# Left-over small runs planned away in a two-layer mixture-of-experts kernel

## Chip, cores and metric

One core of a Trainium2 chip runs the whole program. The metric is the device time of one execution in microseconds, 483.08 us (median of 3 runs, 481.55 to 483.19). Names of engines: PE is TensorE (matmuls; PEld its weight loads), DVE VectorE, ACT ScalarE, POOL GpSimd, SP SyncE, which here only issues DMAs.

## What is computed

The input x is (4, 8, 512, 64) and a state is (4, 8, 32, 64). An attention between them, both ways, gives 4 × (512 + 32) = 2176 tokens of 8 × 64 = 512 numbers. Two mixture-of-experts layers follow, each with 8 experts of hidden width 1024; a token goes to one expert alone, the one with the largest logit.

```python
xread  = softmax(scale * x @ state.T) @ state       # (4, 8, 512, 64)
sread  = softmax(scale * state @ x.T) @ x           # (4, 8, 32, 64)
x = concat([xread, sread], axis=2) -> (2176, 512)

def moe(x, w_gate, w1, w2, capacity=None):
    logits = x @ w_gate                             # (2176, 8)
    e = argmax(logits, axis=1); gate = softmax(logits)[e]
    # with a capacity (576 in layer 0) an expert keeps its first 576 tokens only
    for each expert: y = relu(xe @ w1[e]) @ w2[e];  out[its tokens] = gate * y
```

Everything is fp32. A product is made of three fp32r matmuls, of a high and a low half of either factor (names that end in h and l).

## The kernel before

How many tokens an expert gets is known only on the chip. So each layer first makes a **plan** of runs. A full run, a **quad**, takes 512 rows of one expert: four gathers of 128 rows, turned by PE (`x_quad`), then for each of eight chunks of the hidden width 12 matmuls with w0 (line 1044), relu by ACT into hTh (line 1046) and the low half by DVE into hTl (line 1047), and 12 matmuls with w1 (line 1055). What remains of an expert's rows becomes one more quad where it is over 128 rows, and a **small run** where it is 1 to 128. A small run's rows are turned and copied by ACT at line 1028 and multiplied in plain fp32.

The stages: stage 0 is an expert's first quad; each further quad is a further stage, for which `deeper` opens an `If` on the count of quads (line 1470; the nest goes on to 11 quads). Beside each further stage k, between its matmuls, run up to two small runs, in slots 2(k-1) and 2(k-1)+1. NA is 4, so there are eight such slots. A small run for which there is no place goes into a **left-over slot** (8 to 15) and runs alone after the last quad: `left` tests slot 8's kind (line 1502), and inside it are eight nested tests of the following slots, each with a whole small run in its body. This stands in the program twice, behind either layer.

The plan is a chain of DVE instructions (`plan_runs`, lines 434 to 530). They are emitted a few at a time, by "ticks" between groups of PE's matmuls, in turn with the steps that list the tokens (lov and loc, lines 334 and 336, each read by PE at line 342). Every engine works in order, so PE waits at its list matmuls until DVE has come that far, and a DVE step of the plan that stands ahead of a lov makes it late. `key` orders the remainders by size, `slot` is a small run's place, `nr` holds the counts and kinds that become registers. `m` and `left` in the plan add a jump to slot 8 for those beyond 2 per further stage. `plan_lists` makes the rows to be gathered; its last three instructions make `rows1`, a second list that says which run comes next.

`planned` lets POOL cast nr to integers (line 1518) and issues the next loads of weights; `ready` loads the registers: the count of quads, the kind of the left-over slot (`left_`), the kinds of two small runs. `load_beside` loads the weights of the next small run and branches on whether it is a planned or a left-over one.

The gathers and the stores are indirect DMAs issued by POOL (lines 561 and 1073). The end of an `If` around such DMAs has, on POOL, waits and an instruction that the trace names INC_SWDGE_SEM and the order ISA. Line 1580 is the end of the program.

Of the kernel before, what the change touches and what calls it, by code (L numbers as in the profile page):

```python
# [47 lines left out]
NA = 4  # L48
NS_ = 2 * NA + E
NT = ML * QT + NS_  # L50
# [27 lines left out]
def moe_kernel(ctx: ExitStack, tc: tile.TileContext, x, state, wg1, w1a, w2a, cap, wg2, w1b, w2b, out):  # L78
# [344 lines left out]
    def plan_runs(pool, L):  # L423
# [31 lines left out]
        DVE.scalar_tensor_tensor(out=sm, in0=rem, scalar=0.5, in1=sm, op0=ALU.is_gt, op1=ALU.mult)  # L455
        DVE.tensor_tensor(out=before, in0=before, in1=bc(nl[:, None, :], [P, E, E]), op=ALU.mult)
# [3 lines left out]
        yield  # L460
        start = t_([E], "pst")
        DVE.tensor_reduce(out=start, in_=before, axis=AX.X, op=ALU.add)
        DVE.tensor_tensor(out=key, in0=key, in1=sm, op=ALU.mult)
        kd = t_([E], "pkd")
        DVE.scalar_tensor_tensor(out=kd, in0=rem, scalar=SMALL[0] + 0.5, in1=sm, op0=ALU.is_gt, op1=ALU.add)
        m = t_([2], "pm2")
        DVE.tensor_scalar(m[:, 0:1], nr[:, 0:1], -1.0, float(NA), op0=ALU.add, op1=ALU.min)
        yield
        DVE.tensor_tensor(out=before, in0=bc(key[:, None, :], [P, E, E]), in1=bc(key[:, :, None], [P, E, E]), op=ALU.is_gt)
        DVE.tensor_scalar(m[:, 0:1], m[:, 0:1], 2.0, None, op0=ALU.mult)  # L470
        ends = t_([E], "pen")
# [3 lines left out]
        yield  # L475
        slot = t_([E], "psl")
        DVE.tensor_reduce(out=slot, in_=before, axis=AX.X, op=ALU.add)
        l2 = t_([ML, E], "pl2")
        DVE.tensor_tensor(out=l2, in0=bc(ends[:, None, :], [P, ML, E]), in1=bc(iof[:, 0:ML, None], [P, ML, E]), op=ALU.is_gt)
        DVE.tensor_scalar(m[:, 1:2], m[:, 0:1], -1.0, float(2 * NA), op0=ALU.mult, op1=ALU.add)  # L480
        yield
        left = t_([E], "plf")
        DVE.tensor_scalar(left, slot, m[:, 0:1], m[:, 1:2], op0=ALU.is_ge, op1=ALU.mult)
        DVE.tensor_tensor(out=le, in0=le, in1=l2, op=ALU.mult)
        out_ = t_([E], "pout")
        DVE.tensor_scalar(out_, sm, -FAR, FAR, op0=ALU.mult, op1=ALU.add)
        yield
        DVE.tensor_tensor(out=slot, in0=slot, in1=left, op=ALU.add)
        DVE.tensor_tensor(out=le, in0=le, in1=bc(iof[:, None, 0:E], [P, ML, E]), op=ALU.mult)
        DVE.scalar_tensor_tensor(out=kd, in0=rem, scalar=SMALL[1] + 0.5, in1=kd, op0=ALU.is_gt, op1=ALU.add)  # L490
        yield
        DVE.tensor_tensor(out=slot, in0=slot, in1=out_, op=ALU.add)
        DVE.tensor_reduce(out=nr[:, 1:1 + ML], in_=le, axis=AX.X, op=ALU.add)
        DVE.tensor_tensor(out=kd, in0=kd, in1=sm, op=ALU.mult)
        yield
        se = t_([NS_, E], "pse")
        DVE.tensor_tensor(out=se, in0=bc(slot[:, None, :], [P, NS_, E]), in1=bc(iof[:, 0:NS_, None], [P, NS_, E]), op=ALU.is_equal)
# [18 lines left out]
        DVE.tensor_reduce(out=pr, in_=pk, axis=AX.X, op=ALU.add)  # L516
        no = t_([NA], "pno")
        DVE.tensor_scalar(no, iof[:, 1:1 + NA], nr[:, 0:1], None, op0=ALU.is_ge)
        yield
# [11 lines left out]
        yield  # L531
        rt["plan"] = mk, no

    def plan_lists(pool, L):

        mk, no = rt.pop("plan")
# [11 lines left out]
        yield  # L548
        DVE.tensor_tensor(out=no, in0=no, in1=ss[:, 0:2 * NA].rearrange("p (a b) -> p a b", b=2)[:, :, 0], op=ALU.add)
        yield  # L550
        DVE.tensor_scalar(rows1[L], no, -1.0, 0.0, op0=ALU.add, op1=ALU.max)
        yield

# [479 lines left out]

    def get_next(L, k):
        gather(L, rows1[L][:, k:k + 1], xs1)


# [54 lines left out]
    class Logits:  # L1092
# [22 lines left out]
        def events(self, turns):  # L1115
# [7 lines left out]
            return ev  # L1123

        def alone(self):
            for i in range(0, self.n, 2):
                self.turn(i)
                if i + 1 < self.n:
                    self.turn(i + 1)
                self.product(i, pyv)  # L1130
            return self

# [136 lines left out]

    def load_beside(L, k):  # L1270

        if k >= NA:
            return
        n = load_reg(L, 0, spo, ML)
        with tc.If(n > k + 1) as cmp:
            load_small(L, 2 * k)
        with cmp.Else():
            load_small(L, 2 * NA)

    def split1(half, c):  # L1280
# [4 lines left out]

    nq_, kd_, left_ = {}, {}, {}

# [77 lines left out]
    def stage(L, k, ev=(), ticks=0, fg=()):  # L1365

        lists = [at(SPLIT2, lambda c: wsplit(1, c, ON[4 if L or k else 2])), ev]
        if L or k:
            lists.append(at(SPLITB, split1, 1))
        if k:  # L1370
            lists.append([(SPLITB[-1] + 1, lambda: load_next(L, k + 1, 0)), (SPLIT2[-1] + 1, lambda: load_next(L, k + 1, 1))])
        st = Stage(lists)
        DVE.tensor_copy(mcur, cols(L, k))
        DVE.tensor_copy(gq[0], gq[1])
        if k == 0:
            st.common(CUT[2], ticks, fg)
# [86 lines left out]
    def deeper(st, L, k):  # L1463
# [17 lines left out]
        elif (L, k) in ((0, 2), (1, 0)):  # L1481
            tc.mark_branch_hint_location(f"left{L}", hint="LikelyTaken", engines=ALL)
            tail(st, L, (1, gidx_e[1]) if L == 0 else None)

    def layer(st, L):

        deeper(st, L, 0)
        left(L)

    def left(L):  # L1490

        def alone(s):
            run_all(one(L, 2, s, 0))
            if L == 0:
                run_all(behind(Logits(1, 0).alone()))
            if s + 1 < NS_:
                load_small(L, s + 1)
                get_small(L, s + 1)

        def from_(s):  # L1500
            v = left_[L] if s == 2 * NA else load_reg(L, KINDS + s, mx=len(SMALL))
            with tc.If(v > 0, preferred_fallthrough_block=True, label=f"left{L}" if s == 2 * NA else None):  # L1502
                if L == 0 and s == 2 * NA:
                    run_all(behind(Logits(QT + 2, 0).alone()))
                    nothing(meta[:, 0:QT + 2])
                alone(s)
                if s + 1 < NS_:
                    from_(s + 1)
                if L == 0 and s == 2 * NA:
                    nothing(meta[:, 0:1])  # L1510

        from_(2 * NA)

# [32 lines left out]
    list_clear()  # L1546
    layer(st, 0)

# [7 lines left out]
    ready(1)  # L1556
    layer(st, 1)

# [37 lines left out]
```

## Time and profile before

| what | value |
|---|---|
| runs | 483.08 us median (481.55 to 483.19) |
| profiled execution | 483.41 us, span 481.6 us |
| mean granted clock of TensorE | 0.962 |
| PE | 428.4 us busy, 89% of the span |
| DVE, ACT, POOL | 187.1, 165.8, 199.6 us |
| HBM | 67.70 MB read, 21.52 MB written |

The span is what the profiler saw of the program's instructions; 1.81 us of the execution lie around it. A busy share is an average: whether an engine sets the time is read from the idle time in front of its instructions and from what ended it. A releaser with a q behind the engine's name (DVEq L1502) is an instruction of that engine's own sequencer: a branch, a wait or a semaphore.

### The profile page before, as it was taken

The page shows a single profiled execution, that of the slowest core. Times are in us where ns is not written, and L with a number is a line of the kernel's source. Part 1 is how long each engine was busy: PE and PEld are TensorE (multiplying, and loading weights), DVE is VectorE, ACT ScalarE, POOL GpSimd, SP SyncE. Part 2 cuts the span into 40 slices and gives each one's busy share as a digit, 9 for nine tenths or more (in the row PEclk, how much of TensorE's full clock was granted, in tenths as well). Part 3 has the DMA queues.
Part 4 walks back from the last instruction along what each step waited for, and adds up shares of the span by engine and source line. Part 5 has one row for each costly group of instructions (what it writes and reads, how often), then busy time and mean ns, then how long its engine had stood idle before and what let it go on. Part 6 is the DMA issues. An engine that isn't in the chain of part 4 may idle for free. (4 is left out here: it accounts for less than half of the span.)

```text
span 481.6 us, 8218 instructions
## 1 busy us (share of the span) xinstructions
PE 428.4 (89%) x2757; PEld 310.8 (65%) x2757; DVE 187.1 (39%) x655; ACT 165.8 (34%) x288; POOL 199.6 (41%) x175
## 2 busy tenths in 40 slices
PE   8859577979999899999989889999989999999880
PEld 5647455757875684775775667777646847768760
DVE  7975655897141340041353052971410100411020
ACT  4657355120244411355312245203423113453010
POOL 6531253110814526415443724558524306675011
PEclk9998788997999999999998999999999999999996
DMA  7363639985999975909732300119997858210001
GB/s 236 98 154 85 212 81 301 227 171 196 395 385 333 372 247 192 338 7 342 297 135 83 94 5 3 68 46 354 340 360 267 302 187 276 95 38 2 8 24 66
DMA packets 47354, 89.38 MB, mean 186 GB/s; under 512 B 8592, under 2 KB 21136, under 8 KB 47248
## 3 DMA queue, kind: packets, MB, share of 16 engines
q1 hardware_dynamic: 42128, 72.43, 45.4%
q0 software_dynamic: 5120, 15.76, 9.4%
q8 instruction: 40, 0.66, 0.6%
q14 instruction: 66, 0.54, 0.4%
HBM read 67.70 MB, written 21.52 MB: 185 GB/s over the span
## 5 line engine op out<-in xcount | busy, mean ns | idle before, releaser
L1047 DVE SCALAR_TENSOR_TENSOR hTl<-ph,hTh 128x512 fp32r<-128x512 f32 x48 | 33.2, 691 | 208.1 <-ACT hTh L1046 187.7
L1055 PE MATMUL py<-w1h,hTh 128*128 128x512 f32 x192 | 81.2, 423 | 0.0
L276 POOL TENSOR_TENSOR w1l<-raw,w1h 128x1024 fp32r<-128x1024 f32 x22 | 52.5, 2392 | 61.9 <-ACT w1h L275 61.8
L1055 PE MATMUL py<-w1h,hTl 128*128 128x512 f32 x192 | 75.2, 392 | 0.6 <-issue 0.6
L1055 PE MATMUL py<-w1l,hTh 128*128 128x512 f32 x192 | 75.1, 391 | 0.0
L1046 ACT ACTIVATE hTh<-ph 128x512 fp32r<-128x512 f32 x48 | 28.7, 599 | 131.9 <-PE ph L1044 94.8
L1283 POOL TENSOR_TENSOR w0l<-raw,w0h 128x512 fp32r<-128x512 f32 x40 | 51.1, 1293 | 40.0 <-ACT w0h L1282 39.9
L1044 PE MATMUL ph<-xTh,w0h 128*128 128x512 f32 x192 | 55.2, 410 | 4.8 <-ACTq L1470 1.5
L1044 PE MATMUL ph<-xTl,w0h 128*128 128x512 f32 x192 | 55.4, 410 | 0.0
L1044 PE MATMUL ph<-xTh,w0l 128*128 128x512 f32 x192 | 55.1, 410 | 0.0
L1044 PEld LDWEIGHTS ph<-xTh,w0h 128*128 128x128 f32 x192 | 35.8, 192 | 14.7 <-issue 2.8
L1044 PEld LDWEIGHTS ph<-xTl,w0h 128*128 128x128 f32 x192 | 35.6, 190 | 13.0 <-issue 6.1
L1055 PEld LDWEIGHTS py<-w1h,hTh 128*128 128x128 f32 x192 | 36.1, 188 | 9.4 <-issue 3.4
L1044 PEld LDWEIGHTS ph<-xTh,w0l 128*128 128x128 f32 x192 | 35.8, 194 | 9.5 <-issue 2.5
L1055 PEld LDWEIGHTS py<-w1h,hTl 128*128 128x128 f32 x192 | 36.1, 188 | 8.9 <-issue 1.0
L1055 PEld LDWEIGHTS py<-w1l,hTh 128*128 128x128 f32 x192 | 36.2, 189 | 6.5 <-issue 1.0
L1073 POOL DMA_INDIRECT out_dram<-ysb,dsti x15 | 15.0, 1000 | 60.6 <-ACT ysb L1063 53.6
L1282 ACT CAST w0h<-raw 128x512 fp32r<-128x512 f32 x40 | 23.8, 618 | 14.2 <-DMA raw<-in_moe_w_dram 6.8
L1073 POOL DMA_INDIRECT yrows<-ysb,dsti x16 | 16.2, 1012 | 28.0 <-DVE oc L334 8.0
L275 ACT CAST w1h<-raw 128x1024 fp32r<-128x1024 f32 x24 | 25.1, 1044 | 0.4 <-ACTq L1502 0.4
L861 PE MATMUL pav<-vg,e1T 128*128 128x264 f32 x56 | 18.3, 456 | 0.5 <-ACT xr L862 0.5
L832 POOL TENSOR_TENSOR u<-u,m 128x512 f32<-128x512 f32 x8 | 8.4, 1054 | 22.9 <-ACT xr L862 11.3
(314 smaller groups left out, 598.4 us busy)
## 6 DMA issues: line engine op xcount, KB each, us to landing
raw<-in_moe_w_dram SPq DMA_DIRECT2D x104, 512.0 KB, 7.2
out_dram<-zb SPq DMA_DIRECT2D x2, 2176.0 KB
xrows<-xr SPq DMA_DIRECT2D x16, 256.0 KB, 3.9
yrows<-zeros SPq DMA_DIRECT2D x3, 1026.0 KB
xb<-in_x_dram SPq DMA_DIRECT2D x6, 512.0 KB
yrows<-zeros SPq DMA_DIRECT2D x1, 1282.5 KB
xb<-in_x_dram SPq DMA_DIRECT2D x4, 256.0 KB, 4.0
st<-in_state_dram SPq DMA_DIRECT2D x1, 256.0 KB
```

What stands on the lines that cost most here:

```text
L275: ACT.copy(h, t)
L276: (POOL if on[c] else DVE).tensor_tensor(out=l, in0=t, in1=h.bitcast(F32), op=ALU.subtract)
L832: POOL.tensor_tensor(out=u[o], in0=u[o], in1=bc(m1[o][:, :, None], [P, S // NS, NS]), op=ALU.mult)
L861: PE.matmul(pv[:, a, 0:GW], e1_[b][:, r % 2, a, r // 2], vg[:, b, a], start=True, stop=True)
L1044: PE.matmul(p, w[k][:, 0, c * P:(c + 1) * P], u[:, k], start=(i == 0 and k == 0), stop=(i == 2 and k == NC1 - 1))
L1046: ACT.activation(out=hTh[:, c % 2], in_=p, func=AF.Relu)
L1047: DVE.scalar_tensor_tensor(out=hTl[:, c % 2], in0=p, scalar=0.0, in1=hTh[:, c % 2].bitcast(F32), op0=ALU.max, op1=ALU.subtract)
L1055: PE.matmul(py[t], u[:, c % 2, t * P:(t + 1) * P], w[c // 2][:, c % 2], start=(c == 0 and i == 0), stop=(c == NC2 - 1 and i == 2))
L1073: i = POOL.indirect_dma_start(out=(yrows if L == 0 else out)[:, :], out_offset=bass.IndirectOffsetOnAxis(ap=dsti[:, y:y + 1], axis=0), in_ ...
L1282: ACT.copy(h, t)
L1283: (POOL if ON[half][c] else DVE).tensor_tensor(out=l, in0=t, in1=h.bitcast(F32), op=ALU.subtract)
```

## The change

The plan now counts the small runs less two per further stage (x). With n small runs and q quads, x = round(max(n − 2q, −3)/3 + 1). The x largest small runs are made quads, whose rows beyond those of the small run are empty; their slots go, the others move down by x, and the count of quads rises by x. So no small run is without a place: NS_ falls from 16 to 8 and the lists from 60 to 52 columns. `left`, `from_`, `alone`, `get_next`, `load_beside`, `rows1`, `left_` and the hints on the left-over branch are gone; the next small run is simply slot 2k.

```diff
-NS_ = 2 * NA + E
+NS_ = 2 * NA
-    rows1 = [ctile([P, NA], I32, f"rows1{i}") for i in range(2)]
...
         DVE.tensor_reduce(out=nr[:, 0:1], in_=nl, axis=AX.X, op=ALU.add)
         yield
+        x = t_([1], "px")
+        DVE.tensor_tensor(out=key, in0=key, in1=sm, op=ALU.mult)
+        DVE.tensor_reduce(out=x, in_=sm, axis=AX.X, op=ALU.add)
+        yield
...
+        DVE.scalar_tensor_tensor(out=x, in0=nr[:, 0:1], scalar=-2.0, in1=x, op0=ALU.mult, op1=ALU.add)
+        yield
...
+        DVE.tensor_scalar(x, x, -3.0, 1.0 / 3, op0=ALU.max, op1=ALU.mult)
+        DVE.tensor_scalar(x, x, MAGIC + 1, MAGIC, op0=ALU.add, op1=ALU.subtract)
+        yield
+        padded = t_([E], "ppd")
+        DVE.scalar_tensor_tensor(out=padded, in0=slot, scalar=x[:, 0:1], in1=sm, op0=ALU.is_lt, op1=ALU.mult)
+        DVE.tensor_scalar(slot, slot, x[:, 0:1], None, op0=ALU.subtract)
+        DVE.tensor_tensor(out=nr[:, 0:1], in0=nr[:, 0:1], in1=x, op=ALU.add)
+        yield
+        DVE.tensor_tensor(out=nl, in0=nl, in1=padded, op=ALU.add)
+        DVE.tensor_tensor(out=sm, in0=sm, in1=padded, op=ALU.subtract)
+        yield
...
-        left = t_([E], "plf")
-        DVE.tensor_scalar(left, slot, m[:, 0:1], m[:, 1:2], op0=ALU.is_ge, op1=ALU.mult)
...
-        ss = sel[:, ML * QT:NT]
-        DVE.tensor_scalar(no, no, ss[:, 2 * NA:2 * NA + 1], None, op0=ALU.mult)
...
-    def load_beside(L, k):
...
         def small2(kind):
             yield from one(L, kind - 1, s + 1, NY - 2)
-            load_beside(L, k)
             if k < NA:
-                get_next(L, k)
+                load_small(L, 2 * k)
+                get_small(L, 2 * k)
...
         elif (L, k) in ((0, 2), (1, 0)):
-            tc.mark_branch_hint_location(f"left{L}", hint="LikelyTaken", engines=ALL)
             tail(st, L, (1, gidx_e[1]) if L == 0 else None)
-
-    def layer(st, L):
-
-        deeper(st, L, 0)
-        left(L)
-
-    def left(L):
...
-        from_(2 * NA)
...
         nq_[L] = load_reg(L, 0, mx=ML)
-        left_[L] = load_reg(L, KINDS + 2 * NA, mx=len(SMALL))
         for s in range(2):
             kd_[s] = load_reg(L, KINDS + s, mx=len(SMALL))
-        get_next(L, 0)
-        load_beside(L, 0)
+        get_small(L, 0)
+        load_small(L, 0)
...
-    layer(st, 0)
+    deeper(st, 0, 0)
```

How this moves instructions is shown at three places. The first is DVE's row where layer 0 ends and layer 1 begins. Before (L1061 are the last evictions of layer 0, L1373 the first instruction of layer 1; left out are the bodies of the left-over runs):

```order
L1440 COPY meta<-mcur 128x12
L1061 TENSOR_SCALAR ysb<-py_1168,gq_1153 128x512
L1061 TENSOR_SCALAR ysb<-py_1170,gq_1153 128x512
L1470 UNCONDITIONAL_BRANCH
L1502 COMPARE_AND_BRANCH
L1112 STREAM_TRANSPOSE lg_9391<-pyT 128x64 x3
...
L1502 UNCONDITIONAL_BRANCH x8
L1183 MEMSET meta 128x1
L1184 MEMSET meta 128x1
L1502 UNCONDITIONAL_BRANCH x2
L1373 COPY mcur<-mde_136 128x12
L1374 COPY gq_1153<-gq_1154 128x4
```

After, where L1056, L1447 and L1350 are the lines that were L1061, L1470 and L1373:

```order
L1417 COPY meta<-mcur 128x12
L1056 TENSOR_SCALAR ysb<-py_1166,gq_1151 128x512
L1056 TENSOR_SCALAR ysb<-py_1168,gq_1151 128x512
L1447 UNCONDITIONAL_BRANCH
L1350 COPY mcur<-mde_134 128x12
L1351 COPY gq_1151<-gq_1152 128x4
L1042 SCALAR_TENSOR_TENSOR hTl<-ph_1163,hTh 128x512
```

The test and the 268 rows between it and layer 1 are gone; layer 1's first instruction stands behind the end of `deeper`'s `If`.

The second is POOL's row at the end of the program. Before (L1073 are the stores of the last quad, ISA at L1502 an INC_SWDGE_SEM, L1580 the end):

```order
L1580 BRANCH_PREFETCH_HINT
L1073 DMA out_dram<-ysb,dsti 2176x512 x4
L1502 COMPARE_AND_BRANCH
L1265 UNCONDITIONAL_BRANCH
L1073 DMA out_dram<-ysb,dsti 2176x512
...
L1502 UNCONDITIONAL_BRANCH
L1502 ISA
L1502 UNCONDITIONAL_BRANCH
L1580 ISA
```

After, where L1068 are the stores and L1526 the end:

```order
L1447 UNCONDITIONAL_BRANCH
L1447 ISA
L1447 UNCONDITIONAL_BRANCH
L1068 DMA out_dram<-ysb,dsti 2176x512 x4
L1526 UNCONDITIONAL_BRANCH
L1526 ISA
```

Between the last stores and the end there is no test and no ISA of a join any more.

The third is DVE's row in the plan of layer 0, from the third of five lovs to the fourth. Before (hTl is a low half of the quad beside it; the rest are the plan's steps and the lists'):

```order
L336 TENSOR_SCALAR lov<-iofb,rpp,tidc 128x128
L462 TENSOR_REDUCE pst<-pbf 128x8
L463 TENSOR_TENSOR key<-key,psm 128x8
L465 SCALAR_TENSOR_TENSOR pkd<-prem,psm 128x8
L467 TENSOR_SCALAR pm_1428<-nr 128x1
L334 TENSOR_SCALAR loc<-iofm,rek 128x192
L1047 SCALAR_TENSOR_TENSOR hTl<-ph_1166,hTh 128x512
L469 TENSOR_TENSOR pbf<-key 128x64
L470 TENSOR_SCALAR pm_1428<-pm_1428 128x1
L472 TENSOR_TENSOR pen<-pst,pnl 128x8
L474 TENSOR_TENSOR ple<-pst,iof 128x88
L336 TENSOR_SCALAR lov<-iofb,rpp,tidc 128x128
```

After, with the lines that were L336 and L1047 now L335 and L1042:

```order
L335 TENSOR_SCALAR lov<-iofb,rpp,tidc 128x128
L460 TENSOR_TENSOR key<-key,psm 128x8
L461 TENSOR_REDUCE px<-psm 128x1
L333 TENSOR_SCALAR loc<-iofm,rek 128x192
L1042 SCALAR_TENSOR_TENSOR hTl<-ph_1164,hTh 128x512
L464 TENSOR_TENSOR pah<-key 128x64
L465 SCALAR_TENSOR_TENSOR px<-nr,px 128x1
L335 TENSOR_SCALAR lov<-iofb,rpp,tidc 128x128
```

Ten rows between the two lovs became six; the plan's other steps follow behind the fifth lov. On PE the group of list matmuls that reads these lovs stands three matmuls of L1055 earlier than before.

## Rows read from the trace of the kernel before

**Rows 1.** The head of the page.

```profile
span 481.6 us, 8218 instructions
```

**Rows 2.** By stretch: length; busy PE, PEld, DVE, ACT, POOL; clock, DMA share, GB/s.

```profile
82.00:284.40 202.40, 190.12 (x1104) 136.68 (x1103) 80.18 (x306) 65.77 (x109) 78.30 (x62) 0.97 0.69 230
284.40:468.20 183.80, 175.97 (x898) 127.35 (x898) 49.67 (x161) 56.50 (x91) 84.52 (x63) 1.00 0.44 154
468.20:481.60 13.40, 0.00 (x0) 0.00 (x0) 0.68 (x1) 0.00 (x0) 2.97 (x3) 0.65 0.21 80
```

**Rows 3.** By stretch, lines 1046 (first row) and 1028: length, ACT busy (xinstructions), clock.

```profile
82.00:284.40 202.40, 14.37 (x24) 0.97 0.69 230
...
82.00:284.40 202.40, 2.35 (x4) 0.97 0.69 230
284.40:468.20 183.80, 1.76 (x3) 1.00 0.44 154
```

**Rows 4.** Line 1502, 255 to 300 us: operation, ns min/median/max, starts.

```profile
L1502 DVEq COMPARE_BRANCH  x1: 74/74/74, 284.2 to 284.2; - x1
```

**Rows 5.** Timeline, all engines: start, duration, instruction, idle before.

```profile
284.17 0.75 DVE L1061 TENSOR_SCALAR ysb<-py,gq 128x512 f32<-128x512 f32 x1 [0.63 <-PE py L1055]
...
284.43 1.17 PE L1044 MATMUL ph<-xTh,w0h 128*128 128x512 f32 x4 [0.30 <-PEq L1502]
...
287.19 0.52 PE L1014 MATMUL pyT<-ident,ysb 128*128 128x128 f32 x3 [1.58 <-DVEq L1502]
287.26 0.77 DVE L1373 COPY mcur<-mde 128x12 f32<-128x12 f32 x1 [2.34 <-DVEq L1502]
```

**Rows 6.** Timeline of POOL at the end.

```profile
470.97 0.99 POOL L1073 DMA_INDIRECT out_dram<-ysb,dsti  x1 [0.31 <-issue]
```

**Rows 7.** Line 1502 over the whole span, POOL's queue.

```profile
L1502 POOLq EVENT_SEMAPHORE  x10: 17/43/43, 274.1 to 473.9; - x10
...
L1502 POOLq INC_SWDGE_SEM  x2: 799/1122/1446, 274.9 to 474.0; - x2
```

**Rows 8.** Line 1580, 472 us to the end.

```profile
L1580 SPq EVENT_SEMAPHORE  x14: 17/28/28, 475.4 to 481.6; - x14
...
L1580 POOLq DRAIN  x3: 50/114/5297, 475.5 to 481.3; - x3
L1580 SPq DRAIN  x3: 7/7/13, 476.2 to 481.0; - x3
```

**Rows 9.** Timeline of DVE in the plan of layer 0.

```profile
103.50 2.35 DVE L457 SCALAR_TENSOR_TENSOR key<-prem,desc 128x8 f32<-128x8 f32 x1
...
108.79 0.30 DVE L336 TENSOR_SCALAR lov<-iofb,rpp,tidc 32x128 f16<-32x128 f16 x1
...
109.25 0.15 DVE L490 SCALAR_TENSOR_TENSOR pkd<-prem,pkd 128x8 f32<-128x8 f32 x1
```

**Rows 10.** Timeline of PE there.

```profile
109.14 0.37 PE L342 MATMUL listp<-lov,loc 32*96 32x128 f16 x2 [0.79 <-DVE lov L336]
109.44 2.08 PE L1044 MATMUL ph<-xTh,w0h 128*128 128x512 f32 x4
111.31 1.91 PE L1044 MATMUL ph<-xTh,w0l 128*128 128x512 f32 x4
```

**Rows 11.** The stretch 106.8 to 113.7 us, columns as in Rows 2.

```profile
106.80:113.70 6.90, 4.93 (x14) 3.89 (x15) 6.73 (x44) 0.00 (x0) 0.24 (x1) 0.51 0.10 13
```

**Rows 12.** Timeline of POOL around the plan.

```profile
103.47 2.36 POOL L276 TENSOR_TENSOR w1l<-raw,w1h 128x1024 fp32r<-128x1024 f32 x1 [10.32 <-ACT w1h L275]
111.01 0.24 POOL L1518 CAST ri<-nr 128x44 int32<-128x44 f32 x1 [5.19 <-DVE nr L504]
```

**Rows 13.** Timeline of PE: a small run of layer 0, one of layer 1.

```profile
141.97 2.37 PE L1212 MATMUL pyT<-raw,xTf 128*64 128x512 f32 x10
...
348.88 1.12 PE L1196 MATMUL pyT<-raw,xTf 128*128 128x512 f32 x2 [1.15 <-DMA raw<-in_moe_w_dram]
```

**Rows 14.** Line 1470 over the whole span, PE's queue.

```profile
L1470 PEldq COMPARE_BRANCH  x7: 75/234/3578, 121.7 to 453.1; - x7
```

More of the change, by code (lines that the diff above doesn't have):

```diff
@@ L455, in plan_runs @@
         DVE.scalar_tensor_tensor(out=sm, in0=rem, scalar=0.5, in1=sm, op0=ALU.is_gt, op1=ALU.mult)
-        DVE.tensor_tensor(out=before, in0=before, in1=bc(nl[:, None, :], [P, E, E]), op=ALU.mult)
         DVE.scalar_tensor_tensor(out=key, in0=rem, scalar=float(E), in1=desc, op0=ALU.mult, op1=ALU.add)
@@ L460, in plan_runs @@
         yield
+        x = t_([1], "px")
+        DVE.tensor_tensor(out=key, in0=key, in1=sm, op=ALU.mult)
+        DVE.tensor_reduce(out=x, in_=sm, axis=AX.X, op=ALU.add)
+        yield
+        ahead = t_([E, E], "pah")
+        DVE.tensor_tensor(out=ahead, in0=bc(key[:, None, :], [P, E, E]), in1=bc(key[:, :, None], [P, E, E]), op=ALU.is_gt)
+        DVE.scalar_tensor_tensor(out=x, in0=nr[:, 0:1], scalar=-2.0, in1=x, op0=ALU.mult, op1=ALU.add)
+        yield
+        slot = t_([E], "psl")
+        DVE.tensor_reduce(out=slot, in_=ahead, axis=AX.X, op=ALU.add)
+        DVE.tensor_scalar(x, x, -3.0, 1.0 / 3, op0=ALU.max, op1=ALU.mult)
[9 more added lines that the diff above has]
+        yield
+        DVE.tensor_tensor(out=before, in0=before, in1=bc(nl[:, None, :], [P, E, E]), op=ALU.mult)
+        kd = t_([E], "pkd")
+        DVE.scalar_tensor_tensor(out=kd, in0=rem, scalar=SMALL[0] + 0.5, in1=sm, op0=ALU.is_gt, op1=ALU.add)
         start = t_([E], "pst")
         DVE.tensor_reduce(out=start, in_=before, axis=AX.X, op=ALU.add)
[L463 to L467, printed above, removed]
+        out_ = t_([E], "pout")
+        DVE.tensor_scalar(out_, sm, -FAR, FAR, op0=ALU.mult, op1=ALU.add)
         yield
-        DVE.tensor_tensor(out=before, in0=bc(key[:, None, :], [P, E, E]), in1=bc(key[:, :, None], [P, E, E]), op=ALU.is_gt)
-        DVE.tensor_scalar(m[:, 0:1], m[:, 0:1], 2.0, None, op0=ALU.mult)
         ends = t_([E], "pen")
@@ L475, in plan_runs @@
         yield
-        slot = t_([E], "psl")
-        DVE.tensor_reduce(out=slot, in_=before, axis=AX.X, op=ALU.add)
         l2 = t_([ML, E], "pl2")
         DVE.tensor_tensor(out=l2, in0=bc(ends[:, None, :], [P, ML, E]), in1=bc(iof[:, 0:ML, None], [P, ML, E]), op=ALU.is_gt)
-        DVE.tensor_scalar(m[:, 1:2], m[:, 0:1], -1.0, float(2 * NA), op0=ALU.mult, op1=ALU.add)
+        DVE.tensor_tensor(out=slot, in0=slot, in1=out_, op=ALU.add)
         yield
-        left = t_([E], "plf")
-        DVE.tensor_scalar(left, slot, m[:, 0:1], m[:, 1:2], op0=ALU.is_ge, op1=ALU.mult)
         DVE.tensor_tensor(out=le, in0=le, in1=l2, op=ALU.mult)
[L485 to L489, printed above, removed]
         DVE.scalar_tensor_tensor(out=kd, in0=rem, scalar=SMALL[1] + 0.5, in1=kd, op0=ALU.is_gt, op1=ALU.add)
         yield
-        DVE.tensor_tensor(out=slot, in0=slot, in1=out_, op=ALU.add)
-        DVE.tensor_reduce(out=nr[:, 1:1 + ML], in_=le, axis=AX.X, op=ALU.add)
+        DVE.tensor_tensor(out=le, in0=le, in1=bc(iof[:, None, 0:E], [P, ML, E]), op=ALU.mult)
         DVE.tensor_tensor(out=kd, in0=kd, in1=sm, op=ALU.mult)
         yield
+        DVE.tensor_reduce(out=nr[:, 1:1 + ML], in_=le, axis=AX.X, op=ALU.add)
         se = t_([NS_, E], "pse")
@@ L516, in plan_runs @@
         DVE.tensor_reduce(out=pr, in_=pk, axis=AX.X, op=ALU.add)
-        no = t_([NA], "pno")
-        DVE.tensor_scalar(no, iof[:, 1:1 + NA], nr[:, 0:1], None, op0=ALU.is_ge)
         yield
@@ L531, in plan_runs @@
         yield
-        rt["plan"] = mk, no
+        rt["plan"] = mk
     def plan_lists(pool, L):
-        mk, no = rt.pop("plan")
+        mk = rt.pop("plan")
         la = pool.tile([KH, 2, P], F32, tag="la", name="la")
@@ L544, in plan_lists @@
         yield from list_out(rows[L], md[L], pyv[:, 0:NT], sel, u)
-        ss = sel[:, ML * QT:NT]
-        DVE.tensor_scalar(no, no, ss[:, 2 * NA:2 * NA + 1], None, op0=ALU.mult)
[L548 to L552, printed above, removed]
     wk = ctx.enter_context(tc.tile_pool(name="work", bufs=1))
@@ L1032, in get_small @@
         gather(L, rows[L][:, ML * QT + s:ML * QT + s + 1], xs1)
-    def get_next(L, k):
-        gather(L, rows1[L][:, k:k + 1], xs1)
     def m1_quad(c, after):
@@ L1123, in events @@
             return ev
[L1125 to L1131, printed above, removed]
     def behind(lt, counted=None):
@@ L1268, in load_small @@
                 wload(1, i, W[L][i], e)
-    def load_beside(L, k):
[L1272 to L1278, printed above, removed]
     def split1(half, c):
@@ L1283, in split1 @@
         (POOL if ON[half][c] else DVE).tensor_tensor(out=l, in0=t, in1=h.bitcast(F32), op=ALU.subtract)
-    nq_, kd_, left_ = {}, {}, {}
+    nq_, kd_ = {}, {}
     def cols(L, k):
@@ L1481, in deeper @@
         elif (L, k) in ((0, 2), (1, 0)):
-            tc.mark_branch_hint_location(f"left{L}", hint="LikelyTaken", engines=ALL)
             tail(st, L, (1, gidx_e[1]) if L == 0 else None)
-    def layer(st, L):
-        deeper(st, L, 0)
-        left(L)
-    def left(L):
[L1492 to L1510, printed above, removed]
-        from_(2 * NA)
     def planned(L):
@@ L1556, in moe_kernel @@
     ready(1)
-    layer(st, 1)
+    deeper(st, 1, 0)
 _INS = ['x', 'state', 'moe_w_gate', 'moe_w1', 'moe_w2', 'moe_capacity', 'moe2_w_gate', 'moe2_w1', 'moe2_w2']
```

## Prediction

> **What bounds the kernel now.** I read the page's head first for the span [rows 1], then the busy time of the engines by stage [rows 2], since a stage in which TensorE is full has another price than one in which it waits. The reader is to see that from 82 us on PE is busy for 190.12 of 202.40 us in layer 0 and for 175.97 of 183.80 us in layer 1, and for nothing in the last 13.40 us. The end is therefore PE's work, plus PE's gaps, plus the tail behind its last matmul. An edit pays only if it takes PE work away, closes a gap of PE or shortens that tail.
>
> Next I asked which of the branches that the change touches is taken with these inputs, from the counts of two lines [rows 3]. Each quad runs line 1046 eight times and each small run runs line 1028 once. Line 1046 stands with 24 in either layer (one of two like rows is shown), so each has 24/8 = 3 quads; layer 0 has 4 small runs and layer 1 has 3. With three quads there are two further stages, each with two places: four places, so no small run is left over. Then I read the left-over test's own line, its branches, waits and semaphore work [rows 4, 7], what PE and DVE do around it between the layers [rows 5], and the program's end [rows 6, 8]. Last came the stretches in which the plan is made [rows 9 to 13].
>
> **What the new rule does with these counts.** x is (max(4 − 6, −3))/3 + 1 = 0.33, rounded 0, in layer 0, and (max(3 − 6, −3))/3 + 1 = 0 in layer 1. No small run becomes a quad; PE, ACT and POOL do the same arithmetic in both kernels. What is left is what the code around it costs when it isn't run, and the plan's own steps.
>
> **The test between the layers goes.** DVE's last eviction of layer 0 starts at 284.17, its branch at L1502 is read at 284.2, and its next instruction starts at 287.26: 2.34 us idle, which end with its own queue, not with data [rows 4, 5]. PE waits 0.30 us at 284.43 behind its own branch and 1.58 us at 287.19 for DVE's queue: the four transposes of ysb stand behind DVE's side of the join, although the ysb that they read was finished at 284.17 + 0.75 = 284.92 [rows 5]. In the new order the block behind the test follows directly, so DVE and PE arrive without a jump. Both gaps stand on the path (PE is full on both sides): −1.88 us. The bounds: nothing, if something else ends last in the same place, and −1.88.
>
> The branch's price is told by the rows: DVE, which is sent past 268 rows, loses 2.34 us. The Trainium skill, "Runtime: NRT & Kernel Launch", section "Instruction fetch mechanics", says that fetching ahead goes straight on only, and that a taken branch to a page outside the window stops the engine for a fetch. By that rule the jumps that stay keep their price, and could get one they don't have now, since all code of layer 1 lies elsewhere; that is a rival below.
>
> **The test at the end goes.** POOL issues the last store at 470.97 for 0.99 us [rows 6]. Then it stands at the join: its last wait there, which I take for the one on the last store's landing, starts at 473.9, and INC_SWDGE_SEM at 474.0 takes 1.446 us [rows 7], to 475.46. Then comes a drain of 5.297 us at 475.5, to 480.8, and the closing handshake to 481.6 [rows 8]. SP's last waits start at 475.4 and its first drain at 476.2, long before 480.8, so POOL's drain sets the end. After the change POOL goes from the end of the store, 470.97 + 0.99 = 471.96, to the drain at once, at about 472.05. If the drain takes its 5.3 us wherever it begins, the end comes at 477.35 + 0.8: −3.4 us. The bounds for this, which no row of before shows: 0, if the drain's end hangs on something behind the store that doesn't move; −1.6, if it begins when the landings are in (473.9 instead of 475.5); −6.1, if the long drain belongs to the semaphore work in front of it and, like the other two drains there (50 and 114 ns), takes next to nothing [rows 8]: then the landing at 473.9, SP's waits (475.4 to 476.2, 0.8) and the handshake (0.8) give an end at 475.5. I take −3.4, since the row nearest to it is the drain's own duration, and the engines have nothing else to do there.
>
> **The plan of layer 0.** The chain of the plan is interleaved on DVE with the lists of tokens, for which PE waits in order. In before the fifth lov starts at 108.79 [rows 9] and PE gets its list matmuls at 109.14, after a gap of 0.79 us [rows 10]. In the new order five DVE steps fewer stand ahead of that lov (10 rows become 6 between the third and fourth lov, and one goes ahead of the third); at the 0.15 us of a small step [rows 9] and more PE is served some 0.8 us sooner. Against that three matmuls of L1055 are now behind this wait instead of ahead of it. Four matmuls at the low clock start 1.87 us apart (109.44, 111.31) [rows 10], so three are 1.4 us there and 0.7 us at the full clock. Sum −0.8 + 0.7 to 1.4: I take +0.3. Bounds: the stretch 106.8 to 113.7 has a granted clock of 0.51, so 1.2 GHz, after the gaps before it [rows 11]; if it isn't entered, the 4.93 us of PE work there take half, −2.5; if it lasts once more as long as the 3.4 us in which two groups of L1044 ran, +1.7.
>
> The four further steps of the plan come behind that and make nr late by about 10 operations of 0.15 us, 1.5 us. POOL's cast of nr already waits 5.19 us for it, and behind it stand POOL's and SP's loads of weights; the first matmul that reads such a weight starts at 141.97 without a wait, 31 us later [rows 12, 13]. I cost the delay at nothing; it is covered by that distance, and if there were no slack at all it would be +1.5.
>
> A long DVE step in the plan is the one at 103.50: 2.35 us for 128x8 [rows 9], where the like at 109.25 takes 0.15. The Trainium skill, "GPSIMD Engine Reference", section "Key points", says that GpSimd shares its SBUF interfaces with VectorE and meets it in instructions with two SBUF inputs; the trace agrees, POOL's subtraction runs beside it from 103.47 for 2.36 us [rows 12]. By that rule each of the added two-input steps could cost 2.2 us when a subtraction of POOL's is under way, which speaks against the change. In layer 0 the same step stays at the same place, and the added ones come when POOL has nothing to do before the cast.
>
> **Layer 1's plan and its loads.** Three operations of the second list, one register load of four on each engine, and SP's load with its branch go. PE's largest wait for a weight of a small run is 1.15 us at 348.88 [rows 13]. The loads are issued somewhat sooner; how much of that reaches the landing no row shows. I take −0.4, a third of that wait; bounds 0 and −1.15.
>
> **The sum.** −1.88 + 0.3 − 3.4 − 0.4 = −5.4 us. The profiled execution took 483.41 us, 1.81 more than its span, so 478.0. The median of the runs shown is 483.08, 0.33 under the profiled one; against it the same sum gives 477.7. I say 478.0.
>
> **Rivals.** (A) The drain's end doesn't move: only the join and the plan count, 483.41 − 2.0 = 481.4. For it: nothing but the end of the program waits for the drain, and its length is unlike that of the other drains. Against: POOL's waits at the join are over at 473.9, and the drain is long after them. (A2) The drain waits for the landings: 483.41 − 2.0 − 1.6 = 479.8. For it: the drain is POOL's last work and the stores its last transfers. Against: in before it takes 5.3 us although it begins 1.6 us behind the last landing. (B) The long drain belongs to INC_SWDGE_SEM and goes with it: 483.41 − 2.0 − 6.1 = 475.3. Against it: a second INC_SWDGE_SEM takes 0.799 us between the layers and no such drain follows [rows 7]. (C) Slower: jumps get dearer in the new code. PE's own branches at L1470, seven of them, have a median of 0.234 us and a longest of 3.578 us [rows 14]. At the median they hardly stop it; if five of them came to stop it for 2.34 us, as DVE was stopped at L1502, that is +11.7 − 5.4 = +6.3, 489.7. It decides from (5.4 + 2.4)/5 = 1.6 us each. Against: the blocks that these jumps pass over keep almost all their rows. (D) The rule pads after all, and a small run becomes a quad: at 183.80/3 = 61 us a stage, less the small run's share, some 530. The counts in [rows 3] exclude it but for an error in my reading of the rounding.
>
> **How the numbers follow.** The measurement of this kernel tells about 0.5% (2.4 us) from no change, so faster is below 480.7, slower above 485.5. My forecast 0.50, A2 0.13, B 0.12, A 0.18, C 0.05, D 0.01, and 0.01 for what I haven't seen. Faster: 0.50 + 0.13 + 0.12 = 0.75, less 0.02 for the upper edge of A2, 0.73. Same: A and that edge, 0.20. Slower: C, D and the unseen, 0.07. The range runs from B to A with 0.5 on either side for the spread of runs: 474.8 to 481.9. The forecast's own range, by the plan's bounds and the join's, is 476.0 to 480.0.
>
> **What would show it.** Right: no idle time of DVE and PE at the first instructions of layer 1; no INC_SWDGE_SEM after the last store; a drain of about 5.3 us that begins at once behind it; 24 and 24 of line 1046's successor, 4 and 3 of line 1028's. Wrong: a drain that begins at once and is longer by what it began sooner (A), one that begins about 1.5 us after the store (A2), a short one (B); a new wait of PE behind branches at L1470's successor (C); a fourth quad (D).

## The result, and the profile after

The changed kernel takes 475.47 us (median of 4 runs, 473.7 to 476.21) against 483.13 us for the kernel before: ratio 0.9846, 95% interval 0.9804 to 0.9889, −7.7 us. Two later series of the same file on other chips, e4 and e11 below, gave 0.9898 (0.986 to 0.9935) and 0.9883 (0.9841 to 0.9926), −5.4 and −5.2 us. So it is faster, by 5.2 to 7.7 us, which is less than 2% and yet clear of the noise. Forecast were −5.1 against the median and 474.8 to 481.9 as range; 475.47 lies inside that, and below the narrower 476.0 to 480.0 that I gave for my own forecast alone, in which the two later series (478.53 and 477.64) lie. One run of before beside e10 to e12, in a slower state of the chip (487.93 us), is left out of its median there, 482.85.

The profiled execution took 476.21 us with a span of 474.4. From its page:

```profile
span 474.4 us, 8132 instructions
...
PE 429.0 (90%) x2757; PEld 310.5 (65%) x2757; DVE 187.0 (39%) x655; ACT 165.4 (35%) x288; POOL 199.4 (42%) x175
```

PE is as busy as before (429.0 us against 428.4), so the 7.2 us of the span came out of idle time. Line 1041 (hTh, formerly 1046) and line 1026 (formerly 1028), by stretches for layer 0 and layer 1 (columns: length, ACT's busy time there with its instructions, granted clock, share of DMA, GB/s), first line 1041:

```profile
82.00:282.00 200.00, 14.35 (x24) 0.97 0.68 230
282.00:464.50 182.50, 14.37 (x24) 1.00 0.44 154
```

and line 1026:

```profile
82.00:282.00 200.00, 2.34 (x4) 0.97 0.68 230
282.00:464.50 182.50, 1.76 (x3) 1.00 0.44 154
```

24 and 24, 4 and 3, as in [rows 3]: nothing is padded. At the join between the layers, the timeline (start, duration, instruction, and in brackets the idle time in front where there is any):

```profile
283.20 0.40 PE L1050 MATMUL py<-w1h,hTl 128*128 128x512 f32 x1
283.44 1.09 PE L1039 MATMUL ph<-xTh,w0h 128*128 128x512 f32 x4
...
283.64 0.75 DVE L1056 TENSOR_SCALAR ysb<-py,gq 128x512 f32<-128x512 f32 x1 [0.62 <-PE py L1050]
...
284.30 0.16 DVE L1350 COPY mcur<-mde 128x12 f32<-128x12 f32 x1
284.37 0.60 PE L1012 MATMUL pyT<-ident,ysb 128*128 128x128 f32 x4
```

Where [rows 5] have 0.30, 1.58 and 2.34 us in brackets, nothing stands any more: the transposes of ysb start as the eviction that they read ends (283.64 + 0.75 = 284.39). At the end, POOL's last store and the end's own line:

```profile
467.29 0.98 POOL L1068 DMA_INDIRECT out_dram<-ysb,dsti  x1 [0.30 <-issue]
```

```profile
L1526 SPq EVENT_SEMAPHORE  x14: 17/28/28, 468.8 to 474.4; - x14
...
L1526 POOLq DRAIN  x3: 50/123/8332, 465.3 to 474.2; - x3
L1526 SPq DRAIN  x3: 7/7/13, 471.1 to 473.8; - x3
```

The store ends at 468.27, the span at 474.4: 6.16 us, where [rows 6, 8] give 9.66. No INC_SWDGE_SEM follows the last store any more. The drain now reads 8.332 us and starts at 465.3, before the last two stores have even begun: POOL's sequencer runs ahead of the engine, and the drain's record begins when it is reached. Its end is what counts: 473.58, that is 5.31 us behind the last store. Before, it started when POOL had nothing in front of it and read 5.297.

In the plan of layer 0, PE at its list matmuls and DVE's steps ahead of them:

```profile
103.98 0.27 PE L341 MATMUL listp<-lov,loc 128*96 128x128 f16 x2 [1.89 <-DVE lov L335]
105.33 0.27 PE L341 MATMUL listp<-lov,loc 128*96 128x128 f16 x2 [1.08 <-DVE lov L335]
106.54 0.27 PE L341 MATMUL listp<-lov,loc 32*96 32x128 f16 x2 [0.94 <-DVE lov L335]
```

```profile
101.30 0.15 DVE L455 SCALAR_TENSOR_TENSOR key<-prem,desc 128x8 f32<-128x8 f32 x1
...
101.45 2.48 DVE L335 TENSOR_SCALAR lov<-iofb,rpp,tidc 128x128 f16<-128x128 f16 x1
```

Three gaps of 1.89, 1.08 and 0.94 us, 3.91 in sum, where before had 3.78 (1.49 and 1.50 by its trace, then 0.79 [rows 10]). In the other profiles the sum is 3.74 to 3.93 with the new plan and 3.80 to 3.91 with the old one. The step of 2.35 us in [rows 9] was `key`; that now takes 0.15, and the next step, the third lov, takes 2.48 (2.36 to 2.49 in all seven profiles of the new plan; `key` takes 2.34 to 2.36 in all seven of the old), beside the same subtraction of POOL's:

```profile
101.49 2.38 POOL L275 TENSOR_TENSOR w1l<-raw,w1h 128x1024 fp32r<-128x1024 f32 x1 [10.42 <-ACT w1h L274]
109.70 0.21 POOL L1465 CAST ri<-nr 128x28 int32<-128x28 f32 x1 [5.83 <-DVE nr L512]
```

The last row is the cast of nr. Its start moved from 111.01 [rows 12] by −1.31 us, in a program whose first 82 us were 2.1 us shorter: 0.8 us late, not the 1.5 that I gave it, and the trace lists nobody who waited for it.

**Where the time went.** Starts of ACT's 48 hTh instructions are the same landmarks in all kernels. The table gives stretches of each profile in us: up to the first hTh, the plan's chunk of layer 0 (4th to 5th hTh), the chunk with the second lists (21st to 22nd), the join (24th to 25th), the start of layer 1's further quads (31st to 34th, where weights of small runs are waited for), four late chunks (42nd to 46th), and the last store's end to the end.

| kernel | first | plan | lists | join | weights | late chunks | tail |
|---|---|---|---|---|---|---|---|
| before | 86.38 | 12.67 | 12.87 | 13.33 | 26.90 | 22.02 | 9.66 |
| changed | 84.27 | 12.26 | 14.68 | 11.03 | 24.77 | 22.40 | 6.16 |
| e4, changed again | 86.62 | 12.65 | 12.06 | 11.03 | 24.79 | 22.40 | 6.17 |
| e11, changed again | 83.33 | 12.97 | 14.83 | 11.05 | 27.38 | 22.40 | 6.16 |
| e1, end's test gone | 85.95 | 12.19 | 12.86 | 13.26 | 24.71 | 22.00 | 6.16 |
| e2, join's test gone | 86.53 | 12.14 | 12.63 | 11.05 | 24.62 | 22.00 | 9.66 |
| e3, both gone | 85.45 | 12.63 | 14.58 | 11.06 | 26.68 | 22.00 | 6.16 |
| e5, one body each | 87.44 | 12.20 | 12.75 | 11.39 | 24.62 | 22.00 | 6.16 |
| e6, e3 and direct loads | 86.59 | 12.15 | 13.07 | 11.04 | 24.97 | 22.00 | 6.17 |
| e12, e6 again | 85.53 | 12.19 | 13.48 | 11.04 | 26.47 | 22.00 | 6.17 |
| e7, a POOL step more | 86.61 | 12.27 | 11.55 | 11.03 | 25.23 | 22.38 | 7.14 |
| e8, 32 bytes | 84.78 | 12.08 | 11.53 | 11.04 | 25.48 | 22.32 | 6.17 |
| e10, both tiles | 85.18 | 12.21 | 13.11 | 11.04 | 24.70 | 22.00 | 6.17 |
| e13, one tile | 86.35 | 12.86 | 11.54 | 11.05 | 25.17 | 22.38 | 6.17 |

Three columns follow the edits and have two values each: join, late chunks, tail (a third one only in e5's join, e8's late chunks and e7's tail, at which these edits aim). The other four scatter by 1 to 4 us from one execution to the next, also between executions of the same file. That is why a single pair of profiles (−7.2) must not be split into causes by its differences.

### The profile page after: what moved, and what is told of

Its sections match the earlier page's. It is cut to its first block, busy times and chain, and to the rows that moved or that the text cites. A ratio compares the mean times of both kernels' runs of the same rounds, so it can differ in the third digit from the quotient of the medians.

```text
span 474.4 us, 8132 instructions
## 1 busy us (share of the span) xinstructions
PE 429.0 (90%) x2757; PEld 310.5 (65%) x2757; DVE 187.0 (39%) x655; ACT 165.4 (35%) x288; POOL 199.4 (42%) x175
## 5 line engine op out<-in xcount | busy, mean ns | idle before, releaser
L1042 DVE SCALAR_TENSOR_TENSOR hTl<-ph,hTh 128x512 fp32r<-128x512 f32 x48 | 33.1, 691 | 208.1 <-ACT hTh L1041 197.8
L1068 POOL DMA_INDIRECT out_dram<-ysb,dsti x15 | 15.0, 999 | 62.7 <-ACT ysb L1058 54.5
L1068 POOL DMA_INDIRECT yrows<-ysb,dsti x16 | 16.1, 1004 | 25.5 <-DVE oc L333 8.0
L1199 PE MATMUL pyT<-raw,xTf 128*32 128x256 f32 (+1 forms) x144 | 17.4, 475 | 0.0
```

Source lines behind the costliest of these rows:

```text
L1042: DVE.scalar_tensor_tensor(out=hTl[:, c % 2], in0=p, scalar=0.0, in1=hTh[:, c % 2].bitcast(F32), op0=ALU.max, op1=ALU.subtract)
L1068: i = POOL.indirect_dma_start(out=(yrows if L == 0 else out)[:, :], out_offset=bass.IndirectOffsetOnAxis(ap=dsti[:, y:y + 1], axis=0), in_ ...
L1199: PE.matmul(pyv[q * n:(q + 1) * n, 0:w], xTf[:, c, 0:n], w1[c][:, 0, q * w:(q + 1) * w], start=(c == 0), stop=(c == NC1 - 1))
```

## The experiments

**The two tests, one at a time and both.** The edits of e1_end, e2_join and e3_both to the kernel before; e1 has the last pair of lines, e2 the first, e3 both (each also drops the test's branch hint, not shown):

```diff
-    layer(st, 0)
+    deeper(st, 0, 0)
...
-    layer(st, 1)
+    deeper(st, 1, 0)
```

> The kernel before without the left-over test behind layer 1 (the program's end); the one between the layers, the plan and the loads stay. Theory S (the sum of the prediction): POOL's drain ends 5.3 us behind its last store instead of behind the join's waits and INC_SWDGE_SEM, -3.4 to -3.5 us against before, ratio 0.993; the two gaps of PE at the start of layer 1 (0.30 and 1.58 us) stay. Rival V (it is the code's volume or place that pays, since the first 82 us came out 2.1 us shorter in the changed kernel): less code, so up to 2 us more, -5.5. Rival N (what the first 82 us showed is scatter from one execution to the next): -3.4, with the first matmul of layer 0 somewhere between 81 and 84 us whatever the kernel.

Measured: 480.4 us against 483.95, ratio 0.9922 (0.9896 to 0.9947), −3.6 us between the medians, as all such differences below. The join stays at 13.26 and the tail is 6.16; POOL's drains on the end's line:

```profile
L1581 POOLq DRAIN  x3: 50/120/8333, 465.8 to 474.7; - x3
```

> The kernel before without the left-over test between the layers; the one at the program's end stays. Theory S: the gaps of 0.30 and 1.58 us go, -1.9 us, ratio 0.996; INC_SWDGE_SEM of about 1.4 us and a drain of 5.3 us still stand at the end. Rival V: up to 2 us more, -4. Rival: the transposes of ysb wait for something else in the same place, 0.

Measured: 480.01 us, ratio 0.9924 (0.9898 to 0.9949), −3.9 us; the join is 11.05 and the tail 9.66, with the drain as before:

```profile
L1581 POOLq DRAIN  x3: 50/117/5297, 470.7 to 476.5; - x3
```

> The kernel before without both left-over tests; plan, second list and loads as before. Theory S: -1.9 - 3.4 = -5.3 us, ratio 0.989; what the changed kernel has beyond that (-7.7 in all) is then the plan, the loads or scatter, some 2.4 us. Rival V: -7.4, and nothing is left for the plan and the loads.

Measured: 476.83 us, ratio 0.9862 (0.9827 to 0.9898), −7.1 us. Each test's own stretch changes by its own amount in all kernels and by nothing else: −3.50 us for the end, −2.3 for the join. Theory S holds, and rival V falls by the table's first column: kernels with less code start layer 0 at 83.3 to 87.4 us in no order. The median of e2 is 1.6 us lower than its join explains (−2.3 would be 0.9952, just above the interval). I come back to that below.

> The changed kernel once more. If the -7.7 us of the first runs hold, ratio 0.984; if 2.1 of them were scatter in the first 82 us, -5.6, ratio 0.988, and its first matmul of layer 0 moves from 81.2 us to nearer 83.

Measured: 478.53 us against 483.95, −5.4 us; its first hTh comes at 86.62 (84.27 in the first profile). The 2.1 us of the first 82 us were scatter.

**How far the jump goes.** e5_shallow keeps both tests of before but one body in each, not eight nested ones. A second cut, not shown, takes the loads of the next run's weights and rows (`load_small`, `get_small`) out of that body. It would lose any further left-over run:

```diff
             alone(s)
-            if s + 1 < NS_:
-                from_(s + 1)
```

> The kernel before with both left-over tests, but only one left-over body inside each instead of eight nested ones (further left-over runs would be lost; there are none here). On DVE the rows passed over at the join fall from 268 to about 145, on the other engines in like measure. Theory F (the jump costs because its target is far from what has been fetched): DVE's 2.34 us idle at the join becomes 1 us or less, PE's 1.58 us goes, -1.5 us. Rival J (a taken jump costs that much at any distance): both stay, 0. The end keeps its waits, its INC_SWDGE_SEM and its drain.

Measured: 474.3 us against 482.54, ratio 0.9828 (0.9798 to 0.9857), −8.2 us; I had expected −1.5. On DVE 64 rows are passed over now (I had said 145). At the join:

```profile
285.05 1.17 PE L1044 MATMUL ph<-xTh,w0h 128*128 128x512 f32 x4
...
285.85 0.17 DVE L1373 COPY mcur<-mde 128x12 f32<-128x12 f32 x1 [0.16 <-DVEq L1499]
...
286.06 0.60 PE L1014 MATMUL pyT<-ident,ysb 128*128 128x128 f32 x4
```

PE's two gaps are gone and DVE's 2.34 us are 0.16 (the join is 11.39, 0.35 above the kernels without a test). The short jump is cheap here: theory F. The Trainium skill, "Runtime: NRT & Kernel Launch", section "Instruction fetch mechanics", has the rule, a fetch where the target lies outside the window; these rows agree with it in that the long jump costs and the short one hardly does, though they show neither the window nor the fetch.

What I had not expected is the end. The test's line on POOL's queue, then POOL's last store:

```profile
L1499 POOLq EVENT_SEMAPHORE  x3: 43/43/43, 274.6 to 275.4; - x3
...
L1499 POOLq INC_SWDGE_SEM  x2: 789/1116/1444, 275.5 to 464.9; - x2
```

```profile
466.53 0.99 POOL L1073 DMA_INDIRECT out_dram<-ysb,dsti  x1 [0.30 <-issue]
```

The test, its branch and an INC_SWDGE_SEM of 1.444 us are all still there, and the tail is 6.16 as without them. The INC starts at 464.9, ahead of the last two stores, and runs beside them. Its waits (3 events, the last at 275.4) are all at the first join; before had ten, the last at 473.9, behind the last store [rows 7]. So what cost 3.5 us at the end was not the test but the join behind the deep nest, which waited: 2.05 us from the store's end (471.96) to the INC (474.01), and the 1.446 us of the INC then in the open. That the wait is for the landings of the last stores, I take from its place. In the programs as built, the join behind the nest waits on all eight semaphores of POOL's DMAs; e5's waits on one, that of its body's only such DMA, and the last quad's stores use four others. Whether the depth or the gathers in the body made the difference, one run can't tell.

**What the drain follows.** e7_poolop is the changed kernel with one step of POOL behind the last store:

```diff
     deeper(st, 1, 0)
+    for w in wset[1][1][0:1]:
+        POOL.memset(w.bitcast(F32), 0.0)
```

> The changed kernel with one POOL memset of 128x1024 behind the last store (on a tile that nobody reads any more). Theory W: POOL's drain ends 5.3 us behind the last work of POOL whatever it is, so the end comes later by as long as the memset takes, 1 to 2.4 us. Rival D: the 5.3 us belong to the indirect stores alone (their descriptors), the memset runs inside them, and the time stays. Either way store to end is 6.16 us in the kernels without the test.

Measured: 475.52 us against 482.54, ratio 0.9842 (0.9801 to 0.9883). The step and the drain:

```profile
466.77 0.98 POOL L1068 DMA_INDIRECT out_dram<-ysb,dsti  x1 [0.30 <-issue]
467.73 0.99 POOL L1505 MEMSET w1l<- 128x1024 f32 x1
```

```profile
L1528 POOLq DRAIN  x3: 50/123/9228, 464.8 to 474.6; - x3
```

The memset ends at 468.72, the drain at 464.82 + 9.23 = 474.05, 5.33 us behind it; the tail is 7.14, 0.98 more than without the memset's 0.99. Theory W: the drain ends 5.3 us behind POOL's last work, be it a store or a memset (no other kind was tried), and the 0.99 us more of POOL's work at the end counted in full.

**The late chunks.** In the changed kernel four late chunks take 22.40 us, in before and the six runs of kernels made from it 22.00 to 22.02. e8_after_pad, e10_places and e13_shift move tiles of the changed kernel by unused ones. e10 has both (448 and 480 bytes a partition), e13 only the first, e8 only the second with 8 columns (32 bytes):

```diff
     efirst = [ctile([1, 1], I32, f"efirst{i}") for i in range(2)]
+    pad1 = ctile([P, 112], F32, "pad1")
+    POOL.memset(pad1, 0.0)
...
     ysb = wk.tile([P, NY, ROW], F32, name="ysb")
+    pad2 = wk.tile([P, 120], F32, name="pad2")
+    POOL.memset(pad2, 0.0)
```

> The changed kernel with a tile of 32 bytes a partition, written once and never read, ahead of w1h, w1l, xTh, xTl, hTh and hTl, so that these stand 32 bytes further on, as they stand (by remainder to 64) in the kernel before. In the changed kernel and its repetition eight of nine steady chunks of layer 1's quads take 0.05 to 0.10 us longer (5.52 instead of 5.42 us) than in before and in the three kernels that only lose a test. Theory P (place in SBUF): the chunk goes back to 5.42, and the time is 1.0 to 1.5 us below the changed kernel's, -6.5 to -7.5 us against before. Rival I (the instruction stream, its place or its waits): the chunk stays at 5.52 and the time at the changed kernel's.

Measured: 474.07 us against 482.54, ratio 0.9832 (0.9802 to 0.9863); the late chunks 22.32. One chunk, from the first matmul of one w0 product to that of the next:

```profile
367.03 1.10 PE L1041 MATMUL ph<-xTh,w0h 128*128 128x512 f32 x4
...
372.58 1.10 PE L1041 MATMUL ph<-xTh,w0h 128*128 128x512 f32 x4
```

5.55 us: theory P fails, the remainder to 64 alone isn't it. But 32 bytes did something: over the stretches between hTh starts that scatter little (see e10), e8 takes 1.1 us more than e10 where the changed kernel takes some 2.

> The kernel before without both left-over tests (as e3_both) and also with the changed kernel's direct loads of the next small run in place of load_beside and get_next; the plan and the second list stay. The prediction gave the loads -0.4 us. Theory S: 0 to -0.5 us against e3_both, -5.5 to -6.5 against before. Rival: PE's wait for the small run's weight in layer 1 (1.15 us in before, also there in e3_both, gone in the changed kernel, but gone too in the two kernels with one test) goes because of the loads: it is never seen again and the gain is -1.5. If it is scatter, it can be there or not.

Measured: 473.41 us, ratio 0.981 (0.9775 to 0.9845), −9.1 us; PE's wait for the weights is inside the scatter (24.97).

> e6_loads a second time (old plan, no left-over tests, direct loads), on the chip of e10 and e11. Theory: 1 to 2 us below the changed kernel, since its steady chunks take 5.42 and not 5.52 us; rival: what e6 was below (9.1 against 7.6 to 8.1 us in its call) was scatter, and it equals the changed kernel within 0.5 us.

Measured: 474.94 us against 482.85, ratio 0.9832 (0.9784 to 0.988), −7.9 us, 2.7 below the changed kernel in the same series (e11); the weights' stretch is 26.47 this time, so the wait comes and goes with the same loads.

> The changed kernel a third time, as measure for e10 and e12 on the same chip. By the first two times (-7.7 and -5.4 us) -5 to -8 us against before; steady chunks of layer 1 at 5.52 us; store to end 6.16; no gap at the join.

Measured: 477.64 us, ratio 0.9883, −5.2 us; the late chunks 22.40.

> The changed kernel with two unused tiles (448 and 480 bytes a partition, each written once) so that every tile that PE's quads read or write in SBUF stands at the very address that it has in e6_loads. The 32 bytes of e8 took a steady chunk of layer 1 only from 5.52 to 5.50 us. Theory P2 (place in SBUF, not by its remainder to 64): 5.42 again, and 1 to 2 us less than the changed kernel in this call. Rival I (the instruction stream): 5.52 again and the changed kernel's time. The changed kernel then still runs PE's same matmuls 4 ns apart more than the old plan's program does, for a reason that these runs don't name.

Measured: 474.56 us, ratio 0.9834 (0.9792 to 0.9877), −8.3 us, 3.1 below the changed kernel in the same series (473.07 to 476.35 against 475.47 to 478.41). The same chunk in e11 and then in e10:

```profile
371.96 1.09 PE L1039 MATMUL ph<-xTh,w0h 128*128 128x512 f32 x4
...
377.53 1.09 PE L1039 MATMUL ph<-xTh,w0h 128*128 128x512 f32 x4
```

```profile
367.57 1.08 PE L1043 MATMUL ph<-xTh,w0h 128*128 128x512 f32 x4
...
373.04 1.08 PE L1043 MATMUL ph<-xTh,w0h 128*128 128x512 f32 x4
```

5.57 and 5.47 us, with the same program but for two memsets by POOL: theory P2. Here the place of the tiles in SBUF sets how close PE's matmuls follow one another. Summed over the stretches between hTh starts that differ by at most 0.2 us (42 to 44 of 47), the changed kernel's three profiles take 1.9 to 2.2 us more than e10's.

> The changed kernel with the first of e10's two unused tiles alone (448 bytes a partition, ahead of everything that PE's quads use). All of w0, w1, xT and hT move on by 448 bytes together; their distances from one another stay as in the changed kernel. If the distances between the tiles decide (weights read while the other operand is read), a steady chunk stays at 5.52 us and the time is the changed kernel's, -5.4 to -7.7 against before. If the addresses themselves decide, it is something else, 5.42 where w0's address is what counts (it now stands where it stands in the kernel before), and -8.

Measured: 476.8 us against 483.79, ratio 0.9846 (0.9819 to 0.9873).

```profile
372.86 1.09 PE L1041 MATMUL ph<-xTh,w0h 128*128 128x512 f32 x4
...
378.43 1.09 PE L1041 MATMUL ph<-xTh,w0h 128*128 128x512 f32 x4
```

5.57 us with all of w0, w1, xT and hT moved together, w0 to the very address that it has in before: so w0's address by itself doesn't decide. Two readings are left. Either the distance between w0 with its neighbours and the tiles behind ysb counts (in e10 it is 480 bytes larger, in e8 32), or the address of the tiles behind ysb (in e10 they move by 928 bytes, in e13 by 448, in e8 by 32). That the distance decides is not shown. The products of w1 with hT speak against it as the whole answer: both stand behind ysb and keep their distance in all these kernels, yet in layer 1 the step from w1h with hTh to w1l with hTh takes 227 ns in e10 and 232 in e13, and the next one, to w1h with hTl, 227 and 231 (medians). Which tiles disturb each other, and by what, no run tells.

## Why the prediction was right, and where it wasn't

**No padding**: right; the counts are the same. **The join**: the mechanism was right, the term a little small: −2.3 us in every kernel without a test there, forecast −1.88. The gaps' sum was 1.88, but idle time is counted from the end that the trace gives a matmul, and in a full row the next one starts before that. The last matmul ahead of the join, before:

```profile
283.74 0.39 PE L1055 MATMUL py<-w1h,hTl 128*128 128x512 f32 x1
```

From its start to the w0 product (284.43) are 0.69 us, after 0.24 (283.20 to 283.44); from there to the transposes 2.76 before and 0.93 after. So start to start the two places cost 0.45 and 1.83, 2.28 us in sum, nearly the whole of the 2.30. **The end**: −3.50 in all kernels without the test, forecast −3.4. The drain follows POOL's last work by 5.3 us, as I took it; A, A2 and B are out, since its end neither stays, nor waits for the landings (in e7 it moves with a memset behind the stores), and it doesn't become short. One sign was ill chosen: the drain did become longer by what it began sooner, as I had written for A, because its record begins when the sequencer gets there; only its end tells the theories apart. My place for the cost was right (waits, INC, then drain), but I laid it on the test's being there; e5 shows that the test may stay.

**The plan**: +0.3 forecast. PE's waits at the lists are the same with both plans (3.74 to 3.93 us and 3.78 to 3.91), so the 0.8 us that I took off didn't come; the chunk is 12.08 to 12.97 in the new plan and 12.14 to 12.67 in the old, so the sign of the whole term stays open. (A slip in the bound: the two groups of L1044 ran from 109.44 to 113.02, 3.6 us and not 3.4, which makes it +1.8.) That five steps fewer stand ahead of the lov was true and brought nothing: the 2.4 us beside POOL's subtraction now fall on the lov itself instead of on `key`. (The lov reads one tensor and two columns, so two tensors as inputs aren't needed for that.) I had said that the long step stays at its place and that no added one meets a subtraction, and had not asked which old step moves into it. **The loads**: −0.4 forecast, unsettled; the wait at layer 1's weights is there or not in any kernel (24.6 to 27.4).

**What the sum lacked**: the lists became shorter and a tile went, so everything behind them in SBUF moved, and PE's matmuls got 1.9 to 2.2 us slower in all (22.40 against 22.00 in four chunks). The prediction held that PE, ACT and POOL do the same arithmetic and cost that at nothing; that is the step that failed. **What stays open**: −3.5 − 2.3 + 2.0 is −3.8, and the changed kernel came out at −5.2 to −7.7, so my −5.4 is nearer to the measurement than the shown parts are. That is luck in part: in the two later series the 2 us that I left out and a gain of 1.4 to 1.6 that I can't name nearly cancel, in the first the gain is 3.9. In each of the series the median lies below the sum of its shown parts (join, tail, place), by 0.1 us (e1) to 4.2 (e7). It lies in the stretches that scatter, of which before seems to have the longer ones more often; with one profile to a series I can't show that, nor why. The record gives a lead: the missing part goes by the series. It is 0.1 to 1.6 us for e1 to e4, where before's runs have a median granted clock of 0.962 and these 0.963 to 0.9645, and 2.8 to 4.2 for e5 to e8, where it is 0.959 against 0.965 to 0.9675. (The shorter tail, itself at 0.65 [rows 2], raises the mean by some 0.002, by an estimate of 3.5 us times 0.31 over 480.) That points to the clock in the stretches that scatter, but isn't shown: no run changes the clock alone. **Rival C** is out: the branches at line 1447 stop PE for the same 2.9 us in sum as before.

The experiments lead to a version better than both: e10, the changed kernel with the tiles of its quads where e6 has them, 474.56 us against 477.64 in one series.

## What to carry to other kernels

A branch whose body never runs can cost twice, as it did here: by a long jump over the body (2.34 us of DVE; 0.16 with a short one), and by a join that waits for DMAs still in flight. One body instead of eight nested ones cured both, at the price of the cases beyond the first. POOL's closing drain ran from POOL's last work in all fourteen profiles, so look at work and waits at POOL's end first. When an edit changes the size of an early tile, compare the pace of steady matmuls before and after: place took back some 2 us of what this edit won.

## What the hardware showed unasked

Matmuls of 128x512 in layer 1 follow one another, by medians over the kinds of neighbours, every 226 to 232 ns in before and in e10 and every 228 to 237 in the changed kernel, at the full clock in all; e10 and the changed kernel differ in two unused tiles alone, each written once. And the granted clock in layer 0's second list making differs between executions. The stretch 251 to 256 us (columns: length, busy PE, PEld, DVE, ACT, POOL, then clock), before and then changed:

```profile
251.00:256.00 5.00, 3.50 (x15) 2.82 (x16) 4.17 (x11) 0.00 (x0) 3.36 (x2) 0.76 0.13 48
```

```profile
251.00:256.00 5.00, 4.92 (x15) 3.74 (x15) 2.74 (x11) 0.59 (x1) 2.81 (x3) 0.50 0.25 65
```

0.76 and 0.50 of the full clock, after PE had waited for the lists in both; e7 and e8, with the same plan as the changed kernel, have 1.00 there though e7's PE waits as well (3.21 us busy of the 5), and their chunk is 11.5 us where the changed kernel's first profile has 14.68.
